# Attention taken in units of two key blocks, seven pairs in float32, and the last terms placed last

## The chip, the cores and the metric

The kernel runs on one core of one Trainium2 chip. The time is the device time of one execution in microseconds; the one given is the median of three runs. Beside them stands one profiled execution, whose trace gives every instruction's start and duration. Engine names: PE is TensorE (matmuls; PEld its weight loads), ACT is ScalarE, DVE is VectorE, POOL is GpSimd, SP is the engine that issues the DMA transfers. Each engine works through its own instructions in the order in which they were written; semaphores make an instruction wait for another engine or for a transfer.

## The reference

Attention with a tanh cap over 2 x 12 heads of 448 rows and 64 columns, then two feed-forward layers:

```
scores = q @ k.T / 8;  scores = 30 * tanh(scores / 30)
attn = exp(scores - max);  attn /= attn.sum + 1e-9;  x = attn @ v      # per head
x = heads side by side                                                # 896 x 768
h = maximum(maximum(x @ w1, x @ w2), x @ w3);  y = h @ w_out           # 768 -> 768 -> 768
g = y @ w_in;  g = max(g, 0) + alpha * min(g, 0);  out = g @ w_out2    # 768 -> 2048 -> 768
```

## The kernel before

Everything is held transposed: columns of the model on the 128 partitions, rows of the sequence (448 per batch, two batches) along the free side. A matmul of 448 columns in float32 takes more passes than one in fp32r (float32 rounded to what TensorE multiplies in one pass), so most products are **split**: each operand is a high part, rounded to fp32r, and a low part, the remainder. A product then is three matmuls, high by high, high by low and low by high (`product`, lines 98 to 100).

*Attention* (`fast_attention`) goes through 12 **pairs** of heads. The 448 keys of a head are three blocks of 128 and a rest of 64. Blocks 0, 1 and 2 of a pair are taken for both heads at once, and the two rests stand together in one **shared block** of 128 rows (`None` in `CHUNKS`). For each block, which the code calls a chunk:

- *Scores* (line 260). For blocks 0 to 2 the weights are on half the rows: head 0 on partitions 0 to 63 and head 1 on 64 to 127, since a head has 64 columns. For the shared block the keys are laid out with zeros, so that one matmul on all 128 rows serves both heads. There are two score buffers (`PB`), so scores wait for the tanh of two blocks before.
- *tanh and exp* on ScalarE (lines 266 and 270), each over the block's 896 columns (448 in the shared block).
- In a split pair VectorE rounds the result to `ah` and takes the remainder `al` (`a_high`, `a_low`); in the pairs in `FULL` (every odd one) the float32 result is used as it is.
- *Values* (`weighted`): the product with the values, of all 128 rows, both for blocks 0 to 2 and for the shared block, whose values have zeros or ones in the half that belongs to the other head. Columns of ones beside the values give the sums for the division. A split pair takes three matmuls for each head, a float32 pair one, which the chip carries out as two instructions.

A pair ends with its **normalisation**: ScalarE copies the result out (`e`), a small transfer carries the sums to another layout, VectorE inverts them, two more transfers spread them (`row`, `rb`), VectorE multiplies (line 336), ScalarE rounds to `xh` and VectorE takes the remainder `xl`.

The order on each engine in attention comes from a planner (`planned`): every step is a task with an engine, a cost, the tasks that it waits for and a key (`KEYS`); of the tasks whose planned inputs are there, an engine takes the one with the lowest key. `GATES` says behind which exponentials the first three weights of the experts are decoded in between (weights arrive as 64-bit words; `decoded`, lines 108 to 124, makes the high and low part with two ScalarE and five VectorE operations).

*The experts* (`experts`): for each of six blocks `f` of h, three accumulators are filled, one per weight, from the 2 x 6 parts of x (batch, pair of the batch); the larger of them is split to `hh` and `hl`. For the first `f` the last two parts, pairs 10 and 11, are put behind those of all three weights (`late=2`), since they come out of attention last. Then the *output projection* (`w_out`, in `whole`) takes for each of its six blocks `o` the terms of both batches over the six blocks of h, and last comes `moe2`. From the experts on the matmuls number 648 + 216 + 576 + 576 = 2016.

Of the kernel before, what the change touches and what calls it, by code (L numbers as in the profile page):

```python
# [10 lines left out]
F32 = mybir.dt.float32  # L11
# [19 lines left out]
def attention_moe_moe2(ctx: ExitStack, tc: tile.TileContext, t):  # L31
# [9 lines left out]
    AB, SB, LB, PB = 6, 4, 4, 2  # L41
# [102 lines left out]
    FULL = range(1, PAIRS, 2)  # L144

    def planned(tasks, start):
# [37 lines left out]
    GATES = (20, 27, 44)  # L184

    KEYS = dict(
        Lx=-16, Lv=-12, XKH=-6, XKL=-5, VH=-3, VL=-2.5, TKA=4.2, TKB=4.3, INV=7, NM=8, XH=8.5, XL=9,
        SC=-1.5, TA=-1, EX=0.5, AH=0.6, AL=0.7, PV=4,
# [4 lines left out]
    def fast_attention(xh, xl, pools, begin):  # L193
# [78 lines left out]
        def a_high(i):  # L272
            a = splits[i]
            ah = work.tile([P, 2, S], F32R, name="ah", bufs=SB)[:, : a.shape[1]]
            rounded(ah, a, "DVE")
            splits[i] = a, ah

        def a_low(i):
            a, ah = splits[i]
            al = work.tile([P, 2, S], F32R, name="al", bufs=LB)[:, : a.shape[1]]  # L280
            remainder(al, a, ah)
            splits[i] = ah, al

        def weighted(i):
# [4 lines left out]
            for head in range(2):  # L289
                j = 0 if block is None else head  # L290
                out = pvs[p][:, head, :S]
                start, stop = block == 0, block is None
                cols = slice(head * P, (head + 1) * P)
                if p in FULL:
                    nc.tensor.matmul(out, values(p, "f")[:, c, cols], splits[i][:, j], start=start, stop=stop)  # L295
                    continue
                ah, al = splits[i]
                vh, vl = (values(p, part)[:, c, cols] for part in "hl")
                nc.tensor.matmul(out, vh, ah[:, j], start=start, stop=False)  # L299
                nc.tensor.matmul(out, vh, al[:, j], start=False, stop=False)  # L300
                nc.tensor.matmul(out, vl, ah[:, j], start=False, stop=stop)  # L301
# [65 lines left out]
        splitting = [i for i in range(n) if CHUNKS[i][0] not in FULL]  # L367
        of = [[i for i in range(n) if CHUNKS[i][0] == p] for p in range(PAIRS)]
# [5 lines left out]
        for p in range(PAIRS):  # L374
# [9 lines left out]
            else:  # L384
                transfer(("Lx", p), 0.63, 2.6, past("XKL", p - 2, 0), s0 + KEYS["Lx"], load_qk, p)
                free = past("SC", of[p - 2][-1]) if p > 1 else []
# [15 lines left out]
            for i in of[p]:  # L402
                two = CHUNKS[i][1] is not None
                m = S * (2 if two else 1)
                deps = past("SC", i - 1) + past("TA", i - PB)
                deps += [("XKL", 0, 0 if i == 0 else 1)] if p == 0 else [("XKL", p, 0)]
                add(("SC", i), "PE", 0.75 if two else 0.61, deps, i + KEYS["SC"], scores, i)
                old = i - AB
                free = [] if old < 0 else past("PV", old) if CHUNKS[old][0] in FULL else past("AL", old)
                add(("TA", i), "ACT", 0.9 if two else 0.53, [("SC", i)] + free, i + KEYS["TA"], tanh, i)  # L410
                add(("EX", i), "ACT", 0.93 if two else 0.56, [("TA", i)], i + KEYS["EX"], exp, i)
                if full:
                    deps = [("EX", i)]
                    cost = 1.5
                else:
                    x = splitting.index(i)
                    free = past("PV", splitting[x - SB]) if x >= SB else []
                    add(("AH", i), "DVE", rounding("DVE", m), [("EX", i)] + free, i + KEYS["AH"], a_high, i)
                    free = past("PV", splitting[x - LB]) if x >= LB else []
                    add(("AL", i), "DVE", low(m), [("AH", i)] + free, i + KEYS["AL"], a_low, i)  # L420
                    deps = [("AL", i)]
                    cost = 1.22
                deps = deps + ready_v + past("PV", i - 1)
                deps += past("TKA", p - 2) + past("TKB", p - 2)
                add(("PV", i), "PE", cost, deps, i + KEYS["PV"], weighted, i)
            free = past("NA", p - 2) + past("NB", p - 2)
# [14 lines left out]
        for w, gate in enumerate(GATES):  # L441
            stages = begin(w)
# [264 lines left out]
```

## Time and profile before

| | |
|---|---|
| median of three runs | 541.27 us (539.97 to 541.96) |
| profiled execution | 541.33 us, of it the span from first to last instruction 539.3 us |
| TensorE busy | 527.0 us (98%), 2519 matmuls |
| VectorE busy | 380.6 us (71%) |
| ScalarE busy | 233.2 us (43%) |
| first experts' matmul | at 117.6 us |

A share of busy time is a mean over stages with different limits: attention (up to about 117 us) uses TensorE, ScalarE and VectorE hard, the rest is a long run of matmuls with weights decoded beside it. In the rows further below, times are microseconds from the start of the span; a mean duration is in nanoseconds.

### The profile page before, as it was taken

What the parts mean: (1) busy time and instruction counts of PE and PEld (TensorE: products, weight loads), DVE (VectorE), ACT (ScalarE), POOL (GpSimd) and SP (SyncE); (2) the same over time, 40 slices, a digit from 0 to 9 for tenths busy, and PEclk for the clock granted to TensorE, in tenths of its full rate; (3) what the DMA queues carried; (4) which work ended last, traced back from release to release, by engine and by line L of the source; (5) the groups of instructions that cost most, each with busy time, mean ns of one, the idle gap of its engine ahead of it and who ended that gap; (6) DMA issues with size and microseconds to landing.
All of it is one profiled execution on the core that took longest, in us unless ns stands there. A gap on an engine that the chain in (4) does not pass through costs nothing.

```text
span 539.3 us, 6459 instructions
## 1 busy us (share of the span) xinstructions
PE 527.0 (98%) x2519; PEld 447.4 (83%) x2519; DVE 380.6 (71%) x512; ACT 233.2 (43%) x296; POOL 5.0 (1%) x20
## 2 busy tenths in 40 slices
PE   7999999999999999999999999999999999999995
PEld 3665566579899999999999999999999999999994
DVE  5768899754988767667666899999988665565300
ACT  5989999862444333233333233333333223223110
POOL 3000000000000000000000000000000000000000
PEclk9999999999999999999999999999999999999998
DMA  6456244115355332233333233322333344344001
GB/s 198 139 152 175 69 115 108 36 35 153 117 177 175 118 117 95 93 110 113 118 117 108 68 118 117 117 80 98 108 98 107 108 131 143 107 132 141 1 35 40
DMA packets 27350, 59.19 MB, mean 110 GB/s; under 512 B 14384, under 2 KB 17584, under 8 KB 27312
## 3 DMA queue, kind: packets, MB, share of 16 engines
q1 hardware_dynamic: 27312, 58.69, 35.3%
q8 instruction: 22, 0.36, 0.3%
q14 instruction: 16, 0.13, 0.1%
HBM read 55.85 MB, written 2.80 MB: 109 GB/s over the span
## 4 chain that ended last, share of the span: by engine, by line
PE 88%; ACT 4%; DVE 3%; DMA 2%; issue 1%; DVEq 0%; SPq 0%; ACTq 0%
PE acc L99 25%; PE acc L100 24%; PE acc L98 24%; PE pv L295 5%; PE sc L260 5%; PE pv L299 2%; ACT a L266 2%; PE pv L300 1%; PE pv L301 1%; DMA rb<-row 1%; ACT a L270 1%; DVE rb L336 1%; ACT e L307 1%; DMA cap_t<-in_cap 1%; DVE f L115 1%
## 5 line engine op out<-in xcount | busy, mean ns | idle before, releaser
L82 ACT CAST wh<-f 128x768 fp32r<-128x768 f32 (+1 forms) x58 | 47.2, 814 | 203.4 <-PE acc L99 195.2
L87 DVE TENSOR_TENSOR wl<-f,wh 128x768 fp32r<-128x768 f32 (+1 forms) x58 | 53.6, 925 | 52.5 <-ACT wh L82 52.3
L99 PE MATMUL acc<-xl,wh 128*128 128x448 f32 x216 | 79.0, 366 | 0.7 <-DVE xl L87 0.7
L98 PE MATMUL acc<-xh,wh 128*128 128x448 f32 x216 | 79.2, 367 | 0.0
L100 PE MATMUL acc<-xh,wl 128*128 128x448 f32 x216 | 78.9, 365 | 0.0
L108 ACT ACTIVATE f<-raw 128x768 f32<-128x768 f32 (+1 forms) x58 | 51.1, 881 | 55.0 <-DVE wl L87 39.1
L98 PE MATMUL acc<-yh,wh 128*128 128x448 f32 x192 | 70.7, 368 | 0.0
L99 PE MATMUL acc<-yl,wh 128*128 128x448 f32 x192 | 70.7, 368 | 0.0
L100 PE MATMUL acc<-yh,wl 128*128 128x448 f32 x192 | 70.7, 368 | 0.0
L98 PE MATMUL acc<-gh,wh 128*128 128x448 f32 x192 | 70.7, 368 | 0.0
L99 PE MATMUL acc<-gl,wh 128*128 128x448 f32 x192 | 70.7, 368 | 0.0
L100 PE MATMUL acc<-gh,wl 128*128 128x448 f32 x192 | 70.7, 368 | 0.0
L118 DVE SCALAR_TENSOR_TENSOR f<-raw,f 128x768 int32<-128x768 int32 (+1 forms) x58 | 53.9, 929 | 1.7
L115 DVE SCALAR_TENSOR_TENSOR f<-raw,f 128x768 int32<-128x768 int32 (+1 forms) x58 | 53.8, 928 | 1.4
L110 DVE TENSOR_SCALAR f<-f 128x768 f32<-128x768 f32 (+1 forms) x58 | 31.6, 545 | 25.5 <-ACT f L108 25.5
L266 ACT ACTIVATE a<-sc,s_in 128x896 f32<-128x896 f32 (+1 forms) x48 | 43.7, 918 | 9.6 <-PE sc L260 9.2
L270 ACT ACTIVATE a<-a,cap_t 128x896 f32<-128x896 f32 (+1 forms) x48 | 44.9, 955 | 0.4
L99 PEld LDWEIGHTS acc<-xl,wh 128*128 128x128 f32 x216 | 40.6, 188 | 4.5 <-DVE xl L87 1.1
L98 PEld LDWEIGHTS acc<-xh,wh 128*128 128x128 f32 x216 | 40.6, 188 | 3.4 <-PE pv L295 0.2
L100 PEld LDWEIGHTS acc<-xh,wl 128*128 128x128 f32 x216 | 40.6, 188 | 3.2
L295 PE MATMUL pv<-a,vf 128*128 128x448 f32 x96 | 40.5, 553 | 0.0
L99 PEld LDWEIGHTS acc<-yl,wh 128*128 128x128 f32 x192 | 36.0, 188 | 3.7
(70 smaller groups left out, 757.6 us busy)
## 6 DMA issues: line engine op xcount, KB each, us to landing
raw<-in_w SPq DMA_DIRECT2D x18, 768.0 KB, 4.4
raw<-in_w_in SPq DMA_DIRECT2D x16, 768.0 KB, 4.3
raw<-in_w_out SPq DMA_DIRECT2D x12, 768.0 KB, 4.4
raw<-in_w_out SPq DMA_DIRECT2D x12, 640.0 KB, 3.9
qkd<-in_qk SPq DMA_DIRECT2D x11, 480.0 KB, 3.8
rb<-row SPq DMA_DIRECT2D x24, 112.0 KB, 3.0
out<-ot SPq DMA_DIRECT2D x12, 224.0 KB, 2.8
vd<-in_v SPq DMA_DIRECT2D x6, 256.0 KB, 4.2
```

What stands on the lines that cost most here:

```text
L82: nc.scalar.copy(out=hi, in_=src)
L87: nc.vector.tensor_tensor(out=lo, in0=src, in1=hi.bitcast(F32), op=ALU.subtract)
L98: nc.tensor.matmul(out, wh, xh, start=first and i == 0, stop=False)
L99: nc.tensor.matmul(out, wh, xl, start=False, stop=False)
L100: nc.tensor.matmul(out, wl, xh, start=False, stop=last and i == n - 1)
L108: nc.scalar.activation(out=f, in_=high.bitcast(F32), func=AF.Abs)
L110: nc.vector.tensor_scalar(out=f, in0=f, scalar1=WORD_MIN, scalar2=WORD_MAX, op0=ALU.max, op1=ALU.min)
L115: nc.vector.scalar_tensor_tensor(out=fi, in0=low, scalar=29, in1=fi, op0=ALU.logical_shift_right, op1=ALU.bitwise_or)
L118: nc.vector.scalar_tensor_tensor(out=fi, in0=high, scalar=-0x40000000, in1=fi, op0=ALU.bitwise_and, op1=ALU.bitwise_or)
L266: nc.scalar.activation(out=a, in_=sc, func=AF.Tanh, scale=s_in)
L270: nc.scalar.activation(out=splits[i], in_=splits[i], func=AF.Exp, scale=cap_t)
L295: nc.tensor.matmul(out, values(p, "f")[:, c, cols], splits[i][:, j], start=start, stop=stop)
```

## The change

**Units.** The four blocks of a pair become two units: blocks 0 and 1 (4 x 448 columns) and block 2 with the shared block (3 x 448). Tanh stays per block, but writes into one buffer of four; exponential, rounding and remainder are done once per unit, except that the first two and last two units (`FINE`) have their exponential, and so the values of their first block, in two pieces. The buffers `a`, `ah`, `al` are doubled in size and halved in number (`AB, SB, LB`). The keys are counted in units; the second scores of a unit have a key lower by 1000, so they follow the first as soon as a buffer is free.

**Shared block on half rows.** Its values are taken with weights on 64 rows for each head, and the terms alternate between the heads, so no zeros are needed in them.

**Seven pairs in float32**: pair 0 joins the odd ones.

**Normalisation**: three buffers in place of two for `e` and `rc`.

**Last terms last**: `late=1`, so of the first `f` only pair 11 stands behind the others; and for the first block of `w_out` the terms of hidden block 5 stand behind those of blocks 0 to 4 of both batches. A fourth weight's transfer is issued at the end of attention.

On TensorE, the shared block of a split pair, before (`sc` are scores, `pv` the values' accumulator, `qkh` and `qkl` the high and low part of queries and keys, `vh` and `vl` of values):

```order
L260 MATMUL sc<-qkh,qkl 128x448 x2
L260 MATMUL sc<-qkh 128x448 [waits Activation_49]
L260 MATMUL sc<-qkl,qkh 128x448
L260 MATMUL sc<-qkh,qkl 128x448
L299 MATMUL pv<-ah,vh_136 128x448 [waits DVE_49]
L300 MATMUL pv<-al,vh_136 128x448 [waits DVE_49]
L301 MATMUL pv<-ah,vl_137 128x448
L299 MATMUL pv<-ah,vh_136 128x448
L300 MATMUL pv<-al,vh_136 128x448
L301 MATMUL pv<-ah,vl_137 128x448
```

and now, of pair 2, with the values of block 2 in front of those of the shared block:

```order
L261 MATMUL sc<-qkh 128x448 [waits Activation_49]
L261 MATMUL sc<-qkl,qkh 128x448
L261 MATMUL sc<-qkh,qkl 128x448
L311 MATMUL pv<-ah,vh_136 128x448 [waits DVE_49]
L311 MATMUL pv<-al,vh_136 128x448 [waits DVE_49]
L311 MATMUL pv<-ah,vl_137 128x448
L311 MATMUL pv<-ah,vh_136 128x448
L311 MATMUL pv<-al,vh_136 128x448
L311 MATMUL pv<-ah,vl_137 128x448
L311 MATMUL pv<-ah,vh_136 128x448 x2
L311 MATMUL pv<-al,vh_136 128x448 x2
L311 MATMUL pv<-ah,vl_137 128x448 x2
```

The values of block 2 have moved behind the shared scores, and the six full-row matmuls of the shared values are now pairs on half rows, alternating between the heads.

On ScalarE, the first instructions of attention (tanh writes `a` from `sc`, the exponential reads and writes `a`), before:

```order
L266 ACTIVATE a<-sc,s_in 128x896 x2
L270 ACTIVATE a<-a,cap_t 128x896
L266 ACTIVATE a<-sc,s_in 128x896
L270 ACTIVATE a<-a,cap_t 128x896
L266 ACTIVATE a<-sc,s_in 128x448
L270 ACTIVATE a<-a,cap_t 128x896
L270 ACTIVATE a<-a,cap_t 128x448
L266 ACTIVATE a<-sc,s_in 128x896 x2
```

and now:

```order
L270 ACTIVATE a<-sc,s_in 128x896 x2
L274 ACTIVATE a<-a,cap_t 128x896 x2
L270 ACTIVATE a<-sc,s_in 128x896
L270 ACTIVATE a<-sc,s_in 128x448
L274 ACTIVATE a<-a,cap_t 128x896
L274 ACTIVATE a<-a,cap_t 128x448
L270 ACTIVATE a<-sc,s_in 128x896 x2
```

Two exponentials stand ahead of the third tanh, where one did.

On TensorE, the first block of the output projection (`hh_1268`, `hl_1269` before and `hh_1144`, `hl_1145` now are hidden block 5; each change of `acc` is a new block of the output), before, where 15 matmuls of that projection stand ahead of block 5:

```order
L98 MATMUL acc_2178<-hh_1266,wh 128x448
L99 MATMUL acc_2178<-hl_1267,wh 128x448
L100 MATMUL acc_2178<-hh_1266,wl 128x448
L98 MATMUL acc_2178<-hh_1268,wh 128x448 [waits Activation_49]
L98 MATMUL acc_2229<-hh_1258,wh 128x448 [waits PE_49]
L99 MATMUL acc_2178<-hl_1269,wh 128x448 [waits DVE_49]
L100 MATMUL acc_2178<-hh_1268,wl 128x448
L98 MATMUL acc_2178<-hh_1258,wh 128x448
```

and now, where 30 do:

```order
L98 MATMUL acc_2052<-hh_1142,wh 128x448
L99 MATMUL acc_2052<-hl_1143,wh 128x448
L100 MATMUL acc_2052<-hh_1142,wl 128x448
L98 MATMUL acc_2052<-hh_1144,wh 128x448 [waits Activation_49]
L99 MATMUL acc_2052<-hl_1145,wh 128x448 [waits DVE_49]
L100 MATMUL acc_2052<-hh_1144,wl 128x448
L98 MATMUL acc_2052<-hh_1144,wh 128x448
L99 MATMUL acc_2052<-hl_1145,wh 128x448
```

The wait for the remainder of hidden block 5 has moved from behind batch 0 to behind both batches.

The diff, cut to its core:

```diff
--- before.py
+++ after.py
...
-    AB, SB, LB, PB = 6, 4, 4, 2
+    AB, SB, LB, PB = 3, 2, 2, 2
...
+    UNITS = [4, 3] * PAIRS
+
+    FINE = (0, 1, len(UNITS) - 2, len(UNITS) - 1)
+
+    FULL = [0, 1, 3, 5, 7, 9, 11]
...
-    GATES = (20, 27, 44)
+    GATES = (10, 13, 22, 2 * PAIRS - 1)
...
-            if part != "l":
-                nc.gpsimd.memset(v_[D:, 3, D : 2 * D], 0.0)
-                nc.gpsimd.memset(v_[:D, 3, 2 * D : 3 * D], 0.0)
...
         def tanh(i):
+
             sc = scs.pop(i)
-            a = work.tile([P, 2, S], F32, name="a", bufs=AB)[:, : sc.shape[1]]
-            nc.scalar.activation(out=a, in_=sc, func=AF.Tanh, scale=s_in)
-            splits[i] = a
-
-        def exp(i):
-            nc.scalar.activation(out=splits[i], in_=splits[i], func=AF.Exp, scale=cap_t)
-
...
+            if i % 2 == 0:
+                splits[i // 2] = work.tile([P, 4, S], F32, name="a", bufs=AB)
+            at = i % 2 * 2
+            nc.scalar.activation(out=splits[i // 2][:, at : at + sc.shape[1]], in_=sc, func=AF.Tanh, scale=s_in)
+
+        def exp(u, cols):
+            a = splits[u][:, cols]
+            nc.scalar.activation(out=a, in_=a, func=AF.Exp, scale=cap_t)
+
+        def a_high(u):
+            a = splits[u][:, : UNITS[u]]
+            ah = work.tile([P, 4, S], F32R, name="ah", bufs=SB)[:, : UNITS[u]]
             rounded(ah, a, "DVE")
-            splits[i] = a, ah
-
-        def a_low(i):
-            a, ah = splits[i]
-            al = work.tile([P, 2, S], F32R, name="al", bufs=LB)[:, : a.shape[1]]
+            splits[u] = a, ah
+
...
+        def chunk_weighted(i):
+
             p, block = CHUNKS[i]
             if block == 0:
                 pvs[p] = pvps.tile([P, 2, 512], F32, tag="ps", name="pv")
             c = 3 if block is None else block
...
+            at = i % 2 * 2
+            if p in FULL:
+                terms = [(values(p, "f"), splits[i // 2])]
+            else:
+                (vh, vl), (ah, al) = (values(p, part) for part in "hl"), splits[i // 2]
+                terms = [(vh, ah), (vh, al), (vl, ah)]
+
+            def term(m, head):
+                v_, a_ = terms[m]
+                r = slice(head * D, (head + 1) * D) if block is None else slice(0, P)
+                j = at if block is None else at + head
+                start, stop = block == 0 and m == 0, block is None and m == len(terms) - 1
+                v_ = v_[r, c, head * P : (head + 1) * P]
+                nc.tensor.matmul(pvs[p][:, head, :S], v_, a_[r, j], start=start, stop=stop)
+
+            turns = [(m, head) for m in range(len(terms)) for head in range(2)]
+            for m, head in turns if block is None else sorted(turns, key=lambda x: x[1]):
+                term(m, head)
 
         def taken(p, h):
 
             if h == 0:
-                divisors[p] = small.tile([P, 2, S], F32, name="e"), small.tile([CP, 2, S // CP], F32, name="rc")
+                e = small.tile([P, 2, S], F32, name="e", bufs=3)
+                divisors[p] = e, small.tile([CP, 2, S // CP], F32, name="rc", bufs=3)
             nc.scalar.copy(out=divisors[p][0][:, h], in_=pvs[p][:, h, :S])
...
+            for u in of[p]:
+                even, m = u % 2 == 0, S * UNITS[u]
+                for i in (2 * u, 2 * u + 1):
...
+                    add(("SC", i), "PE", cost, deps, u + KEYS["SC"] - i % 2 * 1000, scores, i)
...
+                if u in FINE:
+                    add(("EA", u), "ACT", 0.93, [("TA", 2 * u)], u + KEYS["EX"] - 0.3, exp, u, slice(0, 2))
...
+                if u in FINE:
+                    first_deps = [("EA", u)] + deps[1:]
+                    add(("PA", u), "PE", 1.6, first_deps, u + KEYS["PV"] - 0.2, weighted, chunks[:1])
+                    deps, chunks, cost = [("EX", u), ("PA", u)], chunks[1:], cost - 1.5
+                add(("PV", u), "PE", cost, deps, u + KEYS["PV"], weighted, chunks)
+            free = past("NA", p - 3) + past("NB", p - 3)
...
             free = [("EX", gate)]
-            transfer(("WL", w), 0.4, 4.2, [("EX", max(0, gate - 8))] + past("W2", w - 2), 1000 + w * 10, step)
+            gate = gate - 4 if w < 3 else gate
+            transfer(("WL", w), 0.4, 4.2, [("EX", max(0, gate))] + past("W2", w - 2), 1000 + w * 10, step)
+            if w == 3:
+                break
             times = (("ACT", 0.8), ("DVE", 1.05), ("DVE", 1.8), ("ACT", 0.8), ("DVE", 0.9))
...
-                    experts(f, weight, xs, hs, accumulator, small, 2 if f == 0 else 0)
+                    experts(f, weight, xs, hs, accumulator, small, 1 if f == 0 else 0)
                 y = tuple(act.tile([P, KD, B, S], F32R, tag=f"a{h}", name=f"y{h}") for h in "hl")
                 for o in range(KD):
                     wh, wl = whole_weights(wpool, t["w_out"][o])
                     acc = accumulator()
-                    for b in range(B):
-                        terms = [((wh[:, k], wl[:, k]), tuple(h_[:, b] for h_ in hs[k])) for k in range(KD)]
-                        product(acc[:, b], terms)
+                    early = KD - 1 if o == 0 else KD
+                    for k0, k1 in ((0, early), (early, KD)):
+                        for b in range(B) if k0 < k1 else ():
+                            terms = [((wh[:, k], wl[:, k]), tuple(h_[:, b] for h_ in hs[k])) for k in range(k0, k1)]
+                            product(acc[:, b], terms, k0 == 0, k1 == KD)
                     split(y[0][:, o], y[1][:, o], acc, "ACT")
```

## Rows read from the trace of the kernel before

**Rows 1.** Windows: busy time (instructions) of each engine by stretch, clock, DMA.
```profile
10.00:110.00 100.00, 96.22 (x449) 60.96 (x448) 81.86 (x132) 93.19 (x123) 0.00 (x0) 1.00 0.44 118
110.00:140.00 30.00, 29.26 (x131) 24.27 (x130) 18.44 (x33) 11.47 (x19) 0.00 (x0) 1.00 0.41 113
150.00:250.00 100.00, 100.00 (x495) 92.69 (x494) 72.51 (x89) 31.93 (x37) 0.00 (x0) 1.00 0.38 126
300.00:400.00 100.00, 100.00 (x486) 90.81 (x485) 91.38 (x106) 35.63 (x40) 0.00 (x0) 1.00 0.31 101
```

**Rows 2.** Chain of waits in attention: start, microseconds, what ran.
```profile
36.23 0.60 PE sc L260 x3
38.05 0.80 PE sc L260 x6
38.85 0.40 PE pv L299
...
40.27 0.80 PE sc L260 x6
41.07 1.70 PE pv L295 x4
...
45.88 1.50 PE pv L295 x4
...
56.12 0.80 PE sc L260 x6
...
67.95 1.41 PE sc L260 x12
```

**Rows 3.** Groups by form: count | busy, mean ns | idle before.
```profile
L270 ACT ACTIVATE a<-a,cap_t 128x896 f32<-128x896 f32 x36 | 37.3, 1047 | 0.4
...
L87 DVE TENSOR_TENSOR al<-a,ah 128x896 fp32r<-128x896 f32 x18 | 19.4, 1080 | 0.3
...
L270 ACT ACTIVATE a<-a,cap_t 128x448 f32<-128x448 f32 x12 | 8.1, 677 | 0.1
```

**Rows 4.** Timeline of the start, and the landing times of the float32 values.
```profile
7.30 1.35 SPq L227 DMA_DIRECT2D vf<-in_v  x2
...
7.58 1.95 ACT L266 ACTIVATE a<-sc,s_in 128x896 f32<-128x896 f32 x2 [3.33 <-PE sc L260]
...
9.42 1.03 ACT L270 ACTIVATE a<-a,cap_t 128x896 f32<-128x896 f32 x1
...
14.47 0.47 PE L260 MATMUL sc<-qkl,qkh 64*128 64x448 f32 x2 [0.50 <-DVE qkl L87]
...
DMA to landing us min/median/max: 4.4/4.8/5.3
```

**Rows 5.** End of attention: timeline of TensorE, and the chain of pair 10.
```profile
111.92 6.17 PE L295 MATMUL pv<-a,vf 128*128 128x448 f32 x16
...
118.21 0.97 ACT e L307 x2
...
124.62 4.67 DMA rb<-row
...
132.64 0.54 DVE xl L87
...
137.87 0.47 PE L99 MATMUL acc<-xl,wh 128*128 128x448 f32 x1 [0.74 <-DVE xl L87]
```

**Rows 6.** Timeline of TensorE around the last hidden block, with a weight load.
```profile
252.28 0.36 PE L99 MATMUL acc<-hl,wh 128*128 128x448 f32 x1
...
253.09 0.37 PE L100 MATMUL acc<-hh,wl 128*128 128x448 f32 x1
...
253.70 0.19 PEld L99 LDWEIGHTS acc<-hl,wh 128*128 128x128 f32 x1 [0.22 <-DVE hl L87]
...
254.21 0.37 PE L98 MATMUL acc<-hh,wh 128*128 128x448 f32 x1
...
255.45 0.37 PE L98 MATMUL acc<-hh,wh 128*128 128x448 f32 x1
```

More of the change, by code (lines that the diff above doesn't have):

```diff
@@ L288, in weighted @@
             c = 3 if block is None else block
[L289 to L301, printed above, removed]
+            at = i % 2 * 2
[14 more added lines that the diff above has]
+                term(m, head)
         def taken(p, h):
             if h == 0:
-                divisors[p] = small.tile([P, 2, S], F32, name="e"), small.tile([CP, 2, S // CP], F32, name="rc")
+                e = small.tile([P, 2, S], F32, name="e", bufs=3)
+                divisors[p] = e, small.tile([CP, 2, S // CP], F32, name="rc", bufs=3)
             nc.scalar.copy(out=divisors[p][0][:, h], in_=pvs[p][:, h, :S])
@@ L366, in fast_attention @@
         n = len(CHUNKS)
-        splitting = [i for i in range(n) if CHUNKS[i][0] not in FULL]
-        of = [[i for i in range(n) if CHUNKS[i][0] == p] for p in range(PAIRS)]
+        splitting = [u for u in range(n // 2) if CHUNKS[2 * u][0] not in FULL]
+        of = [[u for u in range(n // 2) if CHUNKS[2 * u][0] == p] for p in range(PAIRS)]
         for name in ("KIN", "QIN"):
@@ L385, in fast_attention @@
                 transfer(("Lx", p), 0.63, 2.6, past("XKL", p - 2, 0), s0 + KEYS["Lx"], load_qk, p)
-                free = past("SC", of[p - 2][-1]) if p > 1 else []
+                free = past("SC", 2 * of[p - 2][-1] + 1) if p > 1 else []
                 engine, cols = ROUND["QK"], slice(0, QK)
@@ L401, in fast_attention @@
                 ready_v = [("VL", p)]
[L402 to L416, printed above, removed]
+            for u in of[p]:
+                even, m = u % 2 == 0, S * UNITS[u]
+                for i in (2 * u, 2 * u + 1):
+                    deps = past("SC", i - 1) + past("TA", 2 * u - 2) + past("TA", 2 * u - 1)
+                    deps += [("XKL", 0, 0 if i == 0 else 1)] if p == 0 else [("XKL", p, 0)]
+                    cost = 0.71 if CHUNKS[i][1] in (0, 1) else 0.6 if i % 2 == 0 else 0.8
+                    add(("SC", i), "PE", cost, deps, u + KEYS["SC"] - i % 2 * 1000, scores, i)
+                old = u - AB
+                free = [] if old < 0 else past("PV", old) if CHUNKS[2 * old][0] in FULL else past("AL", old)
+                for i in (2 * u, 2 * u + 1):
+                    two = CHUNKS[i][1] is not None
+                    deps = [("SC", i)] + free
+                    add(("TA", i), "ACT", 0.9 if two else 0.53, deps, u + KEYS["TA"] + i % 2 * 0.01, tanh, i)
+                if u in FINE:
+                    add(("EA", u), "ACT", 0.93, [("TA", 2 * u)], u + KEYS["EX"] - 0.3, exp, u, slice(0, 2))
+                cols = slice(2 if u in FINE else 0, UNITS[u])
+                cost = 0.17 + (cols.stop - cols.start) * S / 1200
+                add(("EX", u), "ACT", cost, [("TA", 2 * u), ("TA", 2 * u + 1)], u + KEYS["EX"], exp, u, cols)
+                if not full:
+                    x = splitting.index(u)
@@ L417, in fast_attention @@
                     free = past("PV", splitting[x - SB]) if x >= SB else []
-                    add(("AH", i), "DVE", rounding("DVE", m), [("EX", i)] + free, i + KEYS["AH"], a_high, i)
+                    add(("AH", u), "DVE", rounding("DVE", m), [("EX", u)] + free, u + KEYS["AH"], a_high, u)
                     free = past("PV", splitting[x - LB]) if x >= LB else []
-                    add(("AL", i), "DVE", low(m), [("AH", i)] + free, i + KEYS["AL"], a_low, i)
-                    deps = [("AL", i)]
@@ L422, in fast_attention @@
-                    cost = 1.22
-                deps = deps + ready_v + past("PV", i - 1)
+                    add(("AL", u), "DVE", low(m), [("AH", u)] + free, u + KEYS["AL"], a_low, u)
+                cost = (3.1 if even else 2.7) if full else (2.5 if even else 2.25)
+                deps = [("EX" if full else "AL", u)] + ready_v + past("PV", u - 1)
                 deps += past("TKA", p - 2) + past("TKB", p - 2)
-                add(("PV", i), "PE", cost, deps, i + KEYS["PV"], weighted, i)
@@ L426, in fast_attention @@
-            free = past("NA", p - 2) + past("NB", p - 2)
+                chunks = [2 * u, 2 * u + 1]
+                if u in FINE:
[4 more added lines that the diff above has]
+            free = past("NA", p - 3) + past("NB", p - 3)
@@ L453, in fast_attention @@
             task(*args)
[L454 removed]
+            if name in (("EX", n // 2 - 1), ("AL", splitting[-1]), ("PV", n // 2 - 1), ("DX", PAIRS - 1)):
                 anchors[name[0]] = list(nc.cur_bb.bb.instructions)[-1]
@@ L591, in whole, with begin @@
             xs = [(xh[:, :, b], xl[:, :, b]) for b in range(B)]
-            kept = {}
+            kept, begun = {}, {}
             def weight(f, w):
                 if (f, w) not in kept:
-                    kept[f, w] = whole_weights(wpool, t["w123"][f, :, w])
+                    begin(f, w)
+                for _ in begun[f, w]:
+                    pass
                 return kept[f, w]
-            def begin(w):
-                kept[0, w] = []
-                return weights(wpool, t["w123"][0, :, w], kept[0, w])
+            def begin(f, w):
+                kept[f, w] = []
+                begun[f, w] = weights(wpool, t["w123"][f, :, w], kept[f, w])
+                return begun[f, w]
             behind = []
```

20 lines of the change are left out of this document (10 added, 10 removed).

## The prediction

> **What bounds the kernel now.** I read the windows by stage first, to see which engine is full in which stage; then the chain of waits inside attention, to see what a block costs TensorE; then the groups by form, for ScalarE and VectorE; last the timeline at the start, at the end of attention and around the last hidden block. In attention (10 to 110 us) TensorE is busy 96.2 of 100 us and ScalarE 93.2, so TensorE is the bound and ScalarE stands right behind it; VectorE has 81.9. From 150 us on TensorE is busy in every microsecond, and so the only things that can shorten that part are fewer matmuls (there are the same 2016 before and after) or a closer spacing of them [rows 1]. The clock column is 1.00 in all of these windows.
>
> The chain shows what attention is made of [rows 2]. From 38.05 to 56.12, 18.07 us, it holds one split and one float32 pair. Six score matmuls on half rows cost 0.80, twelve in a row 1.41: the second six cost 0.61, which is 3 x 0.20, since the two heads of a pair of instructions run beside each other. Values of a split block cost 1.41 (38.85 to 40.27) behind half-row scores, but 1.22 in the shared block (36.23 + 0.60 to 38.05), whose scores are on full rows; in float32 it is 1.70 and 1.50. So each change between half-row and full-row weights costs 0.19 to 0.20.
>
> **The change part by part, on TensorE.**
> (a) Changes of rows. Before, each of blocks 0, 1 and 2 has two (scores to values, and back) and the shared block none: six a pair. Now blocks 0 and 1 have their scores together and their values together (two changes), and the second unit has two: into the full rows of the shared scores, and out of them at the shared values, which are on half rows and stand next to the half-row scores of the next unit. Four a pair: 12 pairs x 2 x 0.195 = -4.7 us.
> (b) Shared values of the five pairs that stay split: six full matmuls of 0.20 become three pairs side by side, 1.22 to 0.61: -3.05 us.
> (c) Shared values of the six pairs that were float32 already. One such matmul is two instructions of 0.375 (a block's two heads are x4 in the chain and 1.50). In order they stand head 0, head 0, head 1, head 1, and if instructions start in order only the middle two lie beside each other: three steps, 1.13 for 1.50. Bounds: 1.50 (none) and 0.75 (all). I take 1.13, half way: 6 x 0.37 = -2.25 us, between 0 and -4.5. The Trainium skill (TensorEngine Tiling (Array Packing), Key Properties) says that different tiles execute weight loads and matmuls in parallel; by it the block would take 0.75 and the whole sum would be 2.6 us lower. No row here has a float32 matmul on half rows; the fp32r scores do as the page says.
> (d) Pair 0 goes from split to float32: values 4 x 1.22 = 4.88 become 3 x 1.50 + 1.13 = 5.63: +0.75 us.
> Together -9.25 us of TensorE work.
>
> (e) The start. Before, TensorE runs nearly without a gap from 14.47 on, with the scores of blocks 0 to 3 and the values of block 0 behind it, 4.4 us of work [rows 4]. Now ScalarE does two tanh (to 9.42), two exponentials of 0.94 and one tanh more before a score buffer comes free, at about 12.2; TensorE stands from 10.2 to 12.4, does blocks 4 and 5 to about 13.9 and then the values of pair 0. That is 4.4 us of work at 14.0. The float32 values of pair 0 have to be there by then: their two transfers are issued from 7.30 over 1.35 us and land 4.4 to 5.3 us after issue, at 13 to 14. So nothing is won or lost: 0, between -0.5 and +1.
>
> (f) New stalls in attention. The values of a unit now wait for a cast and a remainder over up to 1792 columns; at 1.08 us for 896 the remainder alone is 2.2 [rows 3]. Between the end of an exponential and its values the order has the scores of the next unit, the values of the unit before and the scores after that, 1.41 + 2.83 + 1.41 = 5.7 us; rounding needs about 3.4 (the cast some 1.2, an estimate from the remainder's half), so one or two other VectorE operations fit in. At pair 6, where weight decoding falls in between, the order puts the scores of two units ahead of the values, and the second must wait for its tanh: 1 to 2 us. Today's idle of 3.8 us in 10 to 110 includes the start. I add 1.5, between 0 and 4.
>
> So attention ends 9.25 - 1.5 = 7.7 us earlier.
>
> (g) The pair that comes last. Before, the experts run 90 matmuls, then wait 0.74 for the x of pair 11 [rows 5]; now 99 stand before it, 1.8 us more, and with three buffers its copies need not wait for pair 9. That wait goes: -0.74. Next late is pair 10, which moves forward to matmul 52, 10.5 us after the experts begin. Its chain took 15 us from the copies (118.21) to the remainder (133.2); now the copies can be made during the values of pair 11, 5.8 us before the experts begin, which would do, but its reciprocal stands on VectorE behind a weight's decoding and the x of pair 9. I take a wait of 1.0, between 0 and 2.5. Net +0.3.
>
> (h) The last hidden block. The first 15 matmuls of the output projection take 3 us, and the remainder of that block comes 0.2 later than they end. Around that wait the spacing of matmuls changes: 252.28 to 253.09 is four steps, 0.2025 each; 254.21 to 255.45 six, 0.2067 [rows 6]. The windows say the same of the long stretches: 495 matmuls in 100 us before, 486 behind [rows 1]. Nothing else differs (same shapes, same clock), and the spacing stays until the end. Of the restarts that the trace has, at 117.6 and 137.87 the close spacing followed, at 253.71 the wide one; this one is a wait of 0.2 us with the pipeline not yet empty. Now 30 matmuls (6.1 us) stand before the terms of the last block, the wait is gone, and I expect the close spacing to go on: 1352 matmuls x 0.0040 = 5.4, and 0.2 for the wait: -5.6 us; between 0 and -5.6.
>
> Sum: -7.7 + 0.3 - 5.6 = -13.0. The profiled execution took 541.33 us (span 539.3 and 2.03 around it), as good as the median of 541.27, so 528.3 us.
>
> **The rivals.**
> - The wide spacing comes anyway, behind the new wait for pair 10 or another short one. For: one of three restarts did it, and VectorE, at 91 of 100 us from 300 to 400, leaves little room for a closer stream. Against: it needs a wait. If it sets in at the output projection, 533.9; with the experts' first matmuls, 648 x 0.0040 = 2.6 more, 536.5.
> - ScalarE becomes the bound. It has 93.2 of 100 us; joining exponentials saves it 0.2 for each of 20 units (two of 448 columns 1.35, one of 896 1.05, less the 0.1 by which neighbours overlap) [rows 3]. With no less idle than today attention ends only 4 us earlier: 532.0. Against it: part of today's idle is waiting for TensorE, which will be earlier.
> - Float32 on half rows runs side by side in full: 7 x 0.375 = 2.6 us less than with (c), 525.7. Against it: half of each pair of instructions would have to start out of turn; for it, that fp32r pairs start together. The page named under (c) is for this case.
> - The half rows bring nothing in float32: 7 x 0.37 = 2.6 more, 530.9.
> - Slower: rounding in units. If VectorE finishes the remainder late in each of the ten split units, TensorE stands behind it in order, ScalarE gets no scores, and nothing else can go ahead. It decides from 1.3 us a unit (13 in all); a query-and-key split (1.8) and a normalisation (2.2) both falling between cast and remainder give 3.4 + 4.0 = 7.4 against 5.7, 1.7 a unit: 528.3 + 17 - 1.5 = 544. Against it: VectorE is at 82 and loses pair 0's rounding, and between casts and remainders the order mostly has one such operation.
>
> **How the numbers follow.** Forecast 0.40, full overlap in float32 0.10, wide spacing 0.28, ScalarE 0.10, no overlap 0.07, slower 0.05. The forecast's own range is 525.5 to 531.5 ((c) to (g) together). The wide spacing reaches to 536.5, with an attention a little worse to 537.5; beyond that lie the slower case and ScalarE together with the wide spacing. Faster by over 0.5% (2.7 us, about what can be told from no change here) means under 538.6: all of the cases but the slower one and a tenth of the rest, 0.89; same 0.07; slower 0.04.
>
> **What would show it.** The first experts' matmul near 110 us, not 117.6, shows (a) to (f); shared float32 values at 1.1 show (c). Windows late in the profile with 495 matmuls in 100 us show (h), 486 disprove it. The matmul of pair 10 with a wait of about 1 us shows (g). If ScalarE is at 97 in attention and TensorE waits for tanh in every unit, the second rival was right; waits of values on the remainder in every split unit show the last.

## The result, and the profile after

The changed kernel takes 533.59 us (median of six, 531.28 to 536.80) against 540.62 for the kernel before (six, 538.99 to 542.23): 7.0 us faster where 13.0 were forecast; the recorded ratio is 0.990 (0.986 to 0.994), the quotient of these two medians 0.987. Ratios leave out executions over 1.5% above the fastest of their kernel, medians keep them. The profiled execution took 534.31 us, its span 532.5. Against the one of before (541.33) the 7.0 us are made up so, all from the two traces:

| part | forecast | in these two executions |
|---|---|---|
| first matmul of the experts (117.58 before) | -7.7 | -3.9 (113.67) |
| waits behind it, until 140 us | +0.3, and -0.2 of (h) | 1.49 + 0.26 for 0.90 + 0.2: +0.65 |
| spacing of the last 1350 matmuls | -5.4 | -5.4 |
| from the last matmul to the end of the span | 0 | 8.4 for 6.5: +1.9 |
| around the span | 0 | -0.3 |

The windows that answer to [rows 1], with three short ones added (columns as there):

```profile
10.00:110.00 100.00, 95.59 (x455) 60.74 (x454) 75.97 (x108) 92.29 (x109) 0.00 (x0) 0.95 0.46 122
10.00:20.00 10.00, 8.11 (x26) 4.38 (x26) 3.61 (x5) 7.75 (x9) 0.00 (x0) 0.66 0.77 221
60.00:70.00 10.00, 7.48 (x41) 4.70 (x41) 9.65 (x14) 9.97 (x13) 0.00 (x0) 0.97 0.21 45
70.00:80.00 10.00, 10.00 (x44) 7.04 (x42) 9.30 (x16) 9.54 (x11) 0.00 (x0) 0.86 0.31 81
150.00:250.00 100.00, 100.00 (x495) 92.68 (x495) 72.57 (x89) 33.27 (x39) 0.00 (x0) 1.00 0.38 125
300.00:400.00 100.00, 100.00 (x495) 92.69 (x494) 94.59 (x111) 36.59 (x41) 0.00 (x0) 1.00 0.31 101
```

The late window has 495 matmuls, as forecast. New is the clock column: 0.95 in attention where it was 1.00, with 0.66 at the start. Its two levels are 1.2 and 2.4 GHz, so TensorE ran at the lower one for much of 10 to 20 us, and again behind 70.

The chain of waits, which answers to [rows 2] and [rows 4]:

```profile
11.26 0.91 ACT a L270
12.21 2.61 PE sc L261 x12
14.82 4.92 PE pv L311 x8
...
25.01 3.20 PE pv L311 x8
...
29.82 2.46 PE pv L311 x8
...
33.49 2.66 PE pv L311 x12
...
37.76 2.01 PE pv L311 x12
```

TensorE's last score before this ended at 10.3; it stood 1.9 us, waiting for ScalarE. Then twelve scores took 2.61 where [rows 2] has 1.41, and the first float32 values 4.92 where the same unit of the next pair takes 3.20: 2.9 us lost to the clock. The odd units show the shared block: 2.46 in float32 is 1.50 for a block, 0.2 for the change of rows and only 0.75 for the shared values.

Pair 6, in the timeline of ScalarE, VectorE and TensorE:

```profile
60.24 1.81 ACT L274 ACTIVATE a<-a,cap_t 128x1792 f32<-128x1792 f32 x1
...
60.40 0.56 DVE L110 TENSOR_SCALAR f<-f 128x768 f32<-128x768 f32 x1 [0.21 <-ACT f L108]
...
64.86 1.09 DVE L84 CAST ah<-a 128x1792 fp32r<-128x1792 f32 x1
...
66.93 2.02 DVE L87 TENSOR_TENSOR al<-a,ah 128x1792 fp32r<-128x1792 f32 x1
...
67.93 0.47 PE L261 MATMUL sc<-qkh 64*128 64x448 f32 x2 [2.50 <-ACT a L270]
...
69.62 0.58 PE L311 MATMUL pv<-ah,vh 128*128 128x448 f32 x1
```

TensorE stood 2.5 us ahead of the scores at 67.93, and what ended that wait was a tanh: ScalarE, busy 9.97 of 10 us, had copies of `e` and a weight's rounding ahead of it. The order is the one that (f) names, scores of two units ahead of pair 6's values. Placing the values first would hardly have helped: the exponential ended at 62.05, but VectorE was decoding a weight and rounded only at 64.86, so the remainder was there only at 68.95. The values behind the gap have 0.58 for one matmul (the unit takes 3.86, not 2.66).

(a) counts six changes of rows a pair before, 72 in all. Over the whole of attention the order of TensorE's matmuls in the two traces has 57 before and 48 after: at the start and behind 67 us two score blocks, or the values of two or three blocks, stood together before already. [rows 2] has one such place (67.95, x12); another, from the chain of before, is three blocks of float32 values in a row, 3 x 1.50:

```profile
79.02 4.51 PE pv L295 x12
```

The end of attention, which answers to [rows 5], in the timeline of ScalarE, SP and TensorE:

```profile
114.60 0.91 ACT L108 ACTIVATE f<-raw 128x768 f32<-128x768 f32 x1 [3.39 <-DMA raw<-in_w]
115.40 0.84 ACT L82 CAST wh<-f 128x768 fp32r<-128x768 f32 x1
116.12 0.55 ACT L322 COPY e<-pv 128x448 f32<-128x448 f32 x1
...
110.67 7.43 SPq L328 DMA_DIRECT2D rc<-e  x3
...
119.32 1.51 SPq L338 DMA_DIRECT2D row<-rc  x2
...
125.80 0.47 PE L98 MATMUL acc<-xh,wh 128*128 128x448 f32 x1 [1.32 <-ACT xh L82]
```

ScalarE waited 3.39 us for the fourth weight, issued early by the new gate, with pair 11's copies and the rounding of pair 9's x queued behind it. The chain goes on from there: pair 9's rounding, its remainder on VectorE, and behind that pair 10's reciprocal, which ended at 119.30, just ahead of pair 10's `row`:

```profile
116.67 0.47 ACT xh L82
117.62 0.62 DVE xl L87
...
119.32 1.69 DMA row<-rc
```

So pair 10 was late by 1.49 us (124.11 to 125.80, less one step).

### The profile page after: what moved, and what is told of

Same layout as the page of the kernel before. It is cut to its first block, busy times and chain, and to the rows that moved or that the text cites. A ratio compares the mean times of both kernels' runs of the same rounds, so it can differ in the third digit from the quotient of the medians.

```text
span 532.5 us, 6371 instructions
## 1 busy us (share of the span) xinstructions
PE 516.3 (97%) x2511; PEld 444.1 (83%) x2511; DVE 371.7 (70%) x482; ACT 228.9 (43%) x276; POOL 3.9 (1%) x12
## 4 chain that ended last, share of the span: by engine, by line
PE 89%; ACT 4%; DMA 3%; DVE 2%; issue 1%; DVEq 0%; ACTq 0%
PE acc L100 25%; PE acc L98 25%; PE acc L99 25%; PE pv L311 9%; PE sc L261 5%; ACT a L270 1%; ACT a L274 1%; DMA raw<-in_w 1%; DMA cap_t<-in_cap 1%; ACT e L322 1%; ACT wh L82 1%; DMA row<-rc 1%; DMA rb<-row 1%; DVE al L87 1%; DVE rb L351 0%
## 5 line engine op out<-in xcount | busy, mean ns | idle before, releaser
L270 ACT ACTIVATE a<-sc,s_in 128x896 f32<-128x896 f32 (+1 forms) x48 | 41.8, 917 | 8.4 <-PE sc L261 8.1
L311 PE MATMUL pv<-a,vf 128*128 128x448 f32 (+1 forms) x112 | 42.8, 574 | 0.0
L274 ACT ACTIVATE a<-a,cap_t 128x1792 f32<-128x1792 f32 (+3 forms) x28 | 39.5, 1421 | 0.5
L100 PEld LDWEIGHTS acc<-gh,wl 128*128 128x128 f32 x192 | 36.1, 188 | 2.9
```

Of the source, the lines that this page charges most:

```text
L100: nc.tensor.matmul(out, wl, xh, start=False, stop=last and i == n - 1)
L270: nc.scalar.activation(out=splits[i // 2][:, at : at + sc.shape[1]], in_=sc, func=AF.Tanh, scale=s_in)
L274: nc.scalar.activation(out=a, in_=a, func=AF.Exp, scale=cap_t)
L311: nc.tensor.matmul(pvs[p][:, head, :S], v_, a_[r, j], start=start, stop=stop)
```

## The experiments

**1. The spacing alone.** b_split is before with the change's `early` lines; a_nosplit is after without them:

```
-                    early = KD - 1 if o == 0 else KD
+                    early = KD
```

> Before, with only the terms of the last h block moved behind those of both halves in the first output block. Theory A (the short wait for the last h block's remainder is what sets the wide matmul spacing from there to the end): the wait of 0.2 us at 253.5 goes, the spacing stays at 0.2027 instead of 0.2067 us, 495 instead of 486 matmuls in 300 to 400, and the time is 540.6 - 5.6 = 535.0. Rival B (the spacing comes from something else, such as the stage or its addresses): 540.6 less at most the 0.2 us of the wait, and 486 matmuls.

> After, with the terms of the first output block in their old order. Theory A: the wait for the last h block's remainder is back, and with it the spacing of 0.2067 us: 533.6 + 5.5 = 539.1. Rival B: 533.6 plus at most 0.3.

The profiles did as A says. A late window of b_split:

```profile
300.00:400.00 100.00, 100.00 (x495) 92.71 (x494) 93.41 (x110) 37.14 (x42) 0.00 (x0) 1.00 0.34 107
```

And two of a_nosplit, ahead of the wait and behind it:

```profile
150.00:250.00 100.00, 100.00 (x495) 92.52 (x494) 73.26 (x90) 32.77 (x38) 0.00 (x0) 1.00 0.37 121
300.00:400.00 100.00, 100.00 (x486) 90.83 (x485) 93.04 (x110) 36.54 (x41) 0.00 (x0) 1.00 0.31 101
```

The times did not: b_split 537.11 (535.65 to 544.50) against 538.91, ratio 0.996 (0.992 to 1.001); a_nosplit 535.45, not 539.1. Both spread over 8 us: eight runs of b_split lie at 535.6 to 539.2 and two at 544.5, and 1920 matmuls x 0.004 = 7.7. So one program has the close spacing in one execution and the wide one in another. Theory A in this form fell; the new one is that every wait of TensorE may settle the spacing anew, one way or the other ("draws" it), and that it then holds until the next.

**2. The start.** a_fill adds, behind the first pair's scores, eight times

```
+ nc.tensor.matmul(out, fills[:, 0], fills[:, 0].unsqueeze(1).to_broadcast([P, 4, P]), start=True, stop=True)
```

a_start moves pair 0's values forward instead; a_six splits pair 0 again and takes its units whole (one run only; `...` marks the rest of a line):

```
- add(("ONE", part, i), "Pool", 1.0, [], i, beside, part, i)                          # a_start
+ add(("ONE", part, i), "Pool", 1.0, [], i + (0 if part == "f" else 9), beside, part, i)
+ free = free + past("Lv", 1) if p > 1 else free
- add(("SC", i), ... u + KEYS["SC"] - i % 2 * 1000, ...)
+ add(("SC", i), ... u + (KEYS["SC"] if u != 2 else -0.9) - i % 2 * 1000, ...)
- FINE = (0, 1, len(UNITS) - 2, len(UNITS) - 1)                                       # a_six
+ FINE = (len(UNITS) - 2, len(UNITS) - 1)
- FULL = [0, 1, 3, 5, 7, 9, 11]
+ FULL = [1, 3, 5, 7, 9, 11]
```

> After, with 8 small matmuls on zeros put behind the first pair's scores, into the accumulator that the values overwrite: TensorE then idles some 0.2 instead of 1.9 us there, and nothing else changes. Theory A (TensorE's idle at 10.3 to 12.2 is what lets its granted clock fall to 0.66 in 10 to 20, which costs 1.2 us in the scores and 1.7 in the values): clock 1.00 in 10 to 20, next scores x12 in 1.4, values x8 in 3.2, time 533.6 - 2.9 = 530.7. Rival B (the clock falls there whatever TensorE does, or ScalarE's chain sets the pace and takes the gain back): 533.6 within 0.8.

> After, with the float32 value buffers set to ones first, pair 0's values loaded ahead of those of pairs 2 and 4, and the first values ahead of pair 1's scores; the planner then also puts pair 6's first values ahead of its second unit of scores. Theory A (the late values and the idle time at the start cost 2 to 4 us): first values near 11 instead of 14.75, clock near 1.00 in 10 to 20, time 530.0. Rival B (what the start gains is lost again, since ScalarE sets the pace until pair 1): 533.6 within 0.8. For pair 6 theory A expects no gain from the swap, as its values wait for VectorE's remainder at 68.95 in either order.

> After, with pair 0 split again, so six float32 pairs, its first two units then whole, and no filling matmuls. Theory A (idle time at the start costs the clock, whatever the pair's type): the first values wait for exponential, rounding and remainder of four blocks until about 14.5, TensorE idles some 4 us behind 10.3, the clock falls below 0.8 in 10 to 20, and the first experts' matmul comes at 113 to 116. Rival B (the clock falls because of pair 0's float32 matmuls): clock 1.00 in 10 to 20.

a_fill, windows and the first matmul of the experts:

```profile
10.00:20.00 10.00, 9.85 (x45) 4.97 (x43) 4.87 (x7) 9.93 (x12) 0.00 (x0) 1.00 0.78 224
60.00:70.00 10.00, 7.52 (x47) 5.37 (x47) 9.94 (x13) 9.93 (x13) 0.00 (x0) 1.00 0.40 98
150.00:250.00 100.00, 100.00 (x485) 90.81 (x485) 71.10 (x88) 31.95 (x37) 0.00 (x0) 1.00 0.37 119
```
```profile
109.37 0.47 PE L98 MATMUL acc<-xh,wh 128*128 128x448 f32 x1
```

With work in the gap the clock stays at 1.00, and the experts begin at 109.37 instead of 113.67: 2.9 us at the start and 1.4 at pair 6, where the gap was 2.36 us and the clock held. The times do not show this gain: the median of four is 534.07, within rival B's 0.8 of 533.6. The profiled run (537.73) drew the wide spacing at its last wait, 134 us (485 in 150 to 250); the other three, 531.74 to 534.54, have mean clocks of 0.990 to 0.994, so the clock may have fallen elsewhere in them, which no trace shows. In a_start the first values came at 10.49 with the clock at 1.00, but a gap of 2.83, waiting for VectorE, ended at 48.38 and the clock was 0.84 in 50 to 60: experts at 111.88, median 532.05 (its profiled run drew the wide spacing too). a_six, with no float32 in pair 0, has the same fall, and so it is the idle time:

```profile
10.00:20.00 10.00, 6.13 (x21) 4.46 (x21) 8.65 (x9) 4.16 (x4) 0.00 (x0) 0.66 0.64 180
```

Its experts begin at 114.74, as theory A had it. Over all profiles: with the eight matmuls at the start the clock was 1.00 in 10 to 20 in six of six, without them and with the idle time (after, a_nosplit, a_kick1, a_six) 0.66 to 0.83 in four of four. At pair 6 it fell behind gaps of 2.50 to 2.98 us in five of five (after, a_nosplit, a_kick1, a_kicks, a_waits), and behind 2.36 (a_fill) or 1.1 to 1.5 (the rest) in none.

**3. Half rows in float32.** a_fullrows (one run) has a_fill's start, zeros in the unused half of the values again, and

```
- r = slice(head * D, (head + 1) * D) if block is None else slice(0, P)
+ r = slice(head * D, (head + 1) * D) if block is None and p not in FULL else slice(0, P)
```

> After, with the 8 filling matmuls, and with the shared block of the seven float32 pairs on full rows again, its other half zeros. Theory A (on half rows the two heads' float32 matmuls overlap fully): the odd units of these pairs go from 2.46 to 3.0 (1.50 for the two blocks' and 1.50 for the shared values, without the change to half rows), the first experts' matmul from 109.4 to 109.4 + 7 x 0.55 = 113.2. Rival B (ScalarE covers it): the units as in A, but the first experts' matmul within 1.5 of 109.4.

The odd float32 units take 3.01 (2.46 in after), and the experts begin at 112.97 instead of 109.37: theory A. Its chain, with an even and an odd unit of pair 0 and the scores behind them:

```profile
13.79 3.21 PE pv L319 x8
...
18.60 3.01 PE pv L319 x8
21.61 1.43 PE sc L264 x11
```

These scores take 1.43, where after has 1.21: the change of rows has only moved there. So half rows save 0.55 + 0.22 a pair, the 0.75 of the shared values, or some 5 us in seven pairs. Theory A's sum left the move out and came near by luck: 3.6 us reached the experts, and the gap at pair 6 was 1.27 instead of 2.36.

**4. What draws the spacing.** a_kicks and a_waits (one run each) have small matmuls of zeros in the row, as the first line has it in a_waits; a_waits makes TensorE wait as well, by the second:

```
+ nc.tensor.matmul(out[:, :64], fills[:, 0], fills[:, 0, :64], start=False, stop=False)
+ nc.vector.scalar_tensor_tensor(out=x, in0=acc, scalar=0.0, in1=x.bitcast(F32), op0=ALU.mult, op1=ALU.add)
```

> After, with the 8 filling matmuls and with 68 small matmuls of zeros by zeros, 2 to 384 columns wide, put inside the accumulations from 190 us on: each adds zero and costs 0.1 to 0.3 us, some 8 to 15 in all, so only the spacing behind each counts. Theory A (the spacing 0.2027 or 0.2067 is drawn anew whenever the regular row of matmuls is broken, and then holds): both spacings occur behind the 68 breaks, several times each, at the same line and stage. Rival B (it is set by which instruction waited, or by the stage): one spacing all through. Rival C (it depends on the length of the break): some widths are followed by 0.2027 each time, others by 0.2067.

> After, with the 8 filling matmuls, and in the first half of the second MLP a VectorE instruction behind each hidden block, which reads the block's last sums and rewrites 28 to 420 columns of an operand of the next block with the same values: TensorE then waits some 0.3 to 0.8 us at each of 15 blocks. Behind half a block one small matmul of zeros, 64 columns. Only the spacing counts: 27 matmuls are seen behind each wait, 27 behind each small matmul. Theory A (a wait draws the spacing, 0.2067 in about one of four): both spacings behind the waits, 3 to 6 times the wide one. Theory A2 (and a small matmul in the row brings the narrow one back): behind the small matmuls 0.2027 each time, after wide ones too. Rival B (the wide spacing belongs to particular instructions or stages): one spacing behind all 15 waits.

In a_kicks the spacing was 0.2027 behind all 68 breaks, whatever their width: a plain break does not draw. In a_waits TensorE waited at 14 of the 15 blocks, and for 3.3 to 3.6 us, not 0.3 to 0.8 (the clock fell with each, one matmul every 0.373 for 3 to 6 us); back at full clock, 5 of the 14 had the wide spacing and 9 the close one, at the same lines. Behind all 16 small matmuls it was close, behind those in the five wide blocks too; in 14 cases only the 8 matmuls up to the next wait show it. (In a_waits the clock's return lies between a wait and the spacing, so it alone does not tell which of the two draws; at 138 and 254 in the other runs the clock was 1.00 throughout.) One of the five, in TensorE's timeline:

```profile
332.78 0.37 PE L104 MATMUL acc<-yl,wh 128*128 128x448 f32 x1
332.99 0.37 PE L105 MATMUL acc<-yh,wl 128*128 128x448 f32 x1
333.20 0.37 PE L101 MATMUL acc<-yh,wh 128*128 128x448 f32 x1
333.40 0.20 PE L95 MATMUL acc<-fills 128*128 128x64 bf16 x1
333.44 0.45 PE L104 MATMUL acc<-yl,wh 128*128 128x448 f32 x1
333.73 0.36 PE L105 MATMUL acc<-yh,wl 128*128 128x448 f32 x1
333.92 0.36 PE L101 MATMUL acc<-yh,wh 128*128 128x448 f32 x1
334.12 0.37 PE L104 MATMUL acc<-yl,wh 128*128 128x448 f32 x1
```

Starts are 0.207 apart ahead of it (the matmul lasts 0.37 each time), about 0.202 behind it, for some 0.12 us of its own. So two such matmuls went into before (b_kick) and one into after (a_kick1), behind the last waits:

> Before, with two matmuls of zeros, 64 columns wide, in the row: one in the second expert group, behind the wait at 137.9, and one in the second output block, behind the wait at 253.7. Theory A2 (a small matmul brings the narrow spacing back): all runs 535.5 to 539, none above 541, the median at 536.8, and 495 matmuls in 300 to 400. Theory A without A2 (only waits draw): two groups of times as for before, 536 to 539 and 541 to 545.

> After as it is, idle start included, with the one matmul of zeros of 64 columns in the second expert group: with b_kick (536.3) it shows what the change is worth once the spacing is 0.2027 in both. Theory A (the start's fall of the clock, the gap at pair 6 and the late pair are what is left of the miss): 531 to 534.5 by the clock of the run, no second group above 536, median 532.7, a gain of 3.6 over b_kick. Rival B (the forecast's attention was right, and the spacing was all of the miss): median 529 or less.

b_kick: ten runs from 535.69 to 539.71, median 536.29, where before, beside them, had 541.72 with 11 of 17 runs at 540.9 to 545.4; ratio 0.995 (0.990 to 0.999). None of the ten lies in the upper group, as theory A2 has it. By the medians that is 5.4 us, by the ratio some 3; which group holds before's median differs from set to set (538.70 to 539.34 beside the other experiments). a_kick1: twelve runs from 531.38 to 536.78, median 533.83, ratio 0.991 (0.988 to 0.995). What is left of its spread goes with the clock: the run of 531.38 has a mean clock of 0.994, that of 536.78 one of 0.983. With the spacing settled in both, the change is worth 2.5 us (measured at two times and on two chips, each beside its own runs of before). Theory A's mechanism held, but its 532.7, its limit of 536 and its gain of 3.6 did not; by the mean clocks, the clock falls more often than I took it to.

**5. The gaps mended.** a_mend is a_fill with

```
- GATES = (10, 13, 22, 2 * PAIRS - 1)
+ GATES = (9, 14, 22)
```

and a_mkick is a_mend with the small matmul in the second group of the experts.

> After, with the 8 filling matmuls at the start, the weight decodes of the attention gated by units 9, 14, 22 in place of 10, 13, 22, and without the fourth weight transfer inside the attention. Theory A (VectorE reaches pair 6's rounding 2.8 us late, because a decode stands ahead of it; and ScalarE waits 3.4 us for the fourth weight tile ahead of the last sums' copies, so that the late pair's operands are late): against a_fill the gap of 2.7 us near 62 goes and the first experts' matmul comes at 106.7 instead of 109.4; the wait for the late pair falls from 2.0 to under 0.5; a run with the spacing 0.2027 takes 531.7 - 4.4 = 527.3. Rival B (ScalarE is full there, so the idle time only moves to a later pair): first experts' matmul within 1 of 109.4, and 529.5 to 531.7.

> The mended kernel (a_mend) with one matmul of zeros, 64 columns wide, in its second expert group, behind the last wait. Theory A2: all runs between 527.8 and 529.5, median 528.3, spacing 0.2027 to the end. Theory A without A2: most at 528.3 and some one in four at 535 to 537.

a_mend: 528.20 (528.16 to 529.12), ratio 0.980 (0.972 to 0.988); a_mkick: 528.64 (528.04 to 528.81, six runs), 0.979 (0.973 to 0.984). Both beat before and after. (That none of a_mkick's six runs is wide says little of the small matmul: none of a_mend's four is.) But in attention theory A fell and rival B held: the experts begin at 109.75, within 1 of 109.4. VectorE's rounding came in time, and the gap only became two, one waiting for VectorE and one for a tanh; ScalarE has 96% of 10 to 100 us in a_fill and in a_mend alike. In a_mend's timeline:

```profile
64.48 0.47 PE L316 MATMUL pv<-al,vh 128*128 128x448 f32 x1 [1.44 <-DVE al L87]
...
85.69 0.47 PE L261 MATMUL sc<-qkh 64*128 64x448 f32 x2 [1.11 <-ACT a L275]
...
118.87 0.47 PE L98 MATMUL acc<-xh,wh 128*128 128x448 f32 x1 [0.55 <-ACT xh L82]
```

The late pair's wait (start to start, less one step) fell from 1.8 to 0.7, not quite to A's 0.5. The clock stayed at 1.00 in every window of attention, and at 0.997 or more in all four runs (0.990 to 0.996 in a_fill's). So what a_mend gains over a_fill comes from the late pair, from the end of the span (6.6 for 8.1), and, as the mean clocks suggest but no trace shows, from fewer falls behind the shorter gaps.

## Why the prediction was wrong

Two steps failed. Idle gaps of TensorE were priced as time alone in (e) and (f), while the clock fell behind them: 2.9 us at the start, 1.2 at pair 6. And (h) read one execution's spacing as a property of the program. Besides, (a) and (c) were mis-sized by 2.9 and 2.6 us in opposite directions: with the clock held (a_fill) the experts began 8.2 us earlier, near the 7.7 of the forecast, which is luck.

- *(a)* mis-sized. In the steady state it is right with *(b)*: a split pair's units take 2.66 + 2.01 and its scores 1.21 + 1.61, 7.49 together; before it was 3 x 1.41 + 1.22 + 3.00 = 8.45. That is -0.96; (a) and (b) gave -1.0. But before had 57 changes of rows, not 72: 9 fewer after, 1.8 us instead of 4.7.
- *(c)* mis-sized, on the good side: shared float32 values take 0.75, not 1.13, 0.37 less for each of seven pairs. This was the third rival. The Trainium skill (TensorEngine Tiling (Array Packing), Key Properties) says that different tiles can execute weight loads and matmuls in parallel. The 2.46 of the odd units and a_fullrows agree with it. With (a) as counted, the work on TensorE fell by 8.9, not 9.25.
- *(e)* failed. I had the idle time nearly right (10.2 to 12.4; it was 10.3 to 12.2) and weighed it as time alone. It was followed by the lower clock and cost 2.9 us more. The Trainium skill (TensorE: Matmul & The Clock Gate, Part 1) says that an idle TensorE falls back to 1.2 GHz and that the number of slow matmuls differs between runs of one kernel. These rows agree with both: 10 to 20 us shows 0.66 in after and 0.83 in a_nosplit and a_kick1, which do the same there.
- *(f)* right in place and wait, pair 6's scores behind their tanh, and not too low as idle time: 8.9 of work and 8.2 of gain (a_fill) leave 0.7 for new stalls, against 1.5. What failed is the clock behind the gap, 1.2 us in after. VectorE was late there too, but a_mend, with VectorE in time, kept the idle time, with ScalarE as full as before.
- *(g)* right in kind: pair 10 waits, 1.49 instead of 1.0, with its reciprocal behind pair 9's x as forecast; that pair 9's x stood behind the early fourth weight I had not seen.
- *(h)* failed as a forecast of the median, though it fits the two profiled executions to 0.1 us. Of the 29 runs of before in these experiments with a mean clock of 0.997 or more, 17 lie at 535.5 to 538.7 and 12 at 540.9 to 542.5: the wide spacing behind 253.7 was about two cases of five, as far as times tell. The change removes that draw but leaves one at 138 that now holds for 1904 matmuls, 7.6 us. By their times and clocks none of the six runs of after drew wide there, where a_fill and a_start did, which helped the median.
- The rest, 1.9 us at the end, stays open. The last instructions are the same, two copies and two transfers; from the last matmul on it was 6.5 to 6.9 in the profiles of before, b_split and b_kick, 7.3 to 8.4 in seven of after's kind, and 6.6 to 7.0 in a_start, a_six, a_mend and a_mkick.

The second rival (ScalarE as the bound) gave 532.0, near what came, but by another way: ScalarE has 92.3 of 100 us, not 97, and TensorE waits for tanh at pair 6, not in every unit. With the clock held (a_fill, a_mend) it has 96%, so little more was to be had from TensorE's work. The sign held. The range held by luck: 533.59 lies outside the forecast's own 525.5 to 531.5 and inside the whole only because that made room for a wide spacing, which did not come.

Not settled: why a restart takes one spacing or the other (behind the wait at the same weight's remainder the first two steps are 0.31 and 0.20 in after, which went on close, and 0.31 and 0.20 in a_fill, which went on wide), and whether each of b_kick's runs was cured or drew well, as its profiled one did.

## What to carry to other kernels

A figure that one trace shows constant over 1300 instructions may still be one draw: hold it against the spread of the times before counting on it. Count what a change removes over the whole stage, not in one steady stretch of it. Price an idle gap of TensorE by what its clock does behind it, not by its length alone; work that fills the gap can hold the clock although it computes nothing. And where transfers or decodes are issued earlier, look at what stands behind them on the engine that must then wait.

## What the runs showed of the hardware

- Alternating weight loads and matmuls of 448 columns in fp32r have two steady spacings, 0.2027 and 0.2067 us, at full clock. A wait may lead to either (5 of 14 wide in a_waits); a matmul of 64 columns in the row led back to 0.2027 in 5 of 5 cases (8 matmuls seen behind each), and the 68 breaks of a_kicks never led away from it. With two of them in before, none of ten runs lies in the upper group, where 11 of 17 did (median 541.72 to 536.29, ratio 0.995).
- TensorE's granted clock fell behind idle gaps well inside a running kernel: 1.9 us at the start of attention (0.66 to 0.83 in 10 to 20 us), 2.5 to 3.0 at pair 6 (0.83 to 0.97 in 60 to 70, 0.86 to 1.00 in 70 to 80). Eight filling matmuls kept it at 1.00 at the start, in six profiles of six.
- Float32 matmuls of two heads on the two halves of the rows, written one head behind the other, run fully beside each other: 0.75 for both instead of 1.50.
